# A scan with two MLPs on one core: the weights' VectorE work two stages behind ScalarE's, chunk inputs loaded at a period's front, a new token block's low parts and first products later

## The chip, the cores and the metric

The kernel runs on one core of a Trainium2 chip. Its engines run their own instruction streams in the order in which the program issues them: TensorE (PE; weight loads stand apart as PEld), VectorE (DVE), ScalarE (ACT), GpSimd (POOL) and SyncE (SP), which here issues nearly all DMA transfers. The metric is device time in microseconds (us) of one execution; lower is better.

## The reference

Three parts follow one another. A recurrence with a 40 x 40 state for each of 32 heads runs over 768 tokens; its output is the input of two MLPs with hidden width 2048 over 3072 tokens.

```python
for t in range(S):                               # B, H, S, D = 4, 8, 768, 40
    y[:, :, t] = np.einsum('bhd,bhde->bhe', rt, state)
    Sa = np.einsum('bhde,bhe->bhd', state, at)
    state_decay = state * wt[:, :, None, :] - np.einsum('bhd,bhe->bhde', Sa, bt)
    state = state_decay + np.einsum('bhd,bhe->bhde', vt, kt)
x = y.transpose(0, 2, 1, 3).reshape(B * S, H * D)        # 3072 x 320
h = x @ w_in                                     # 320 x 2048
x = (np.maximum(h, 0.0) ** 2) @ w_out            # 2048 x 320
h = x @ w_in2
out = (h * np.cos(h)) @ w_out2
```

The MLP weights come as 64-bit patterns of doubles and are turned into single precision on the chip.

## The kernel before, in words

**Chunks and periods.** The recurrence is cut into 12 chunks of 64 tokens. For each chunk the interaction of its tokens is a triangular system per head, which is solved; then the state moves on by matrix products. `Program.period(c)` is one period: a table of 42 slots says, with `at(slot, function, ...)`, what is issued when. Everything in a slot is written out in program order, and each engine takes its share in that order; nothing is reordered later.

A period holds work of several chunks. For chunk c, the state's products (`pq`, `px`, `pu`, `py`, `pm`) and the stores. For chunk c+1, the end of `gt` (products `pgt` on PE, masked by DVE into `ga`), `gt_out` (SP writes `ga` to DRAM as `Ls`, L445), `solve_load` in slot 6 (SP loads `T`, L458, and four pieces of `L` back from `Ls`, L461, then two `l`, L463), the solver from slot 9 to 36, `solve_store` (Tn, Ts) in slot 37 and `load_t` in slot 38. For chunk c+2, the inputs: `load_kb` (L362, the k and b inputs, 832 KB, into tile `cin`), `load_a` (L365, tile `at`), `compact_kb` (DVE multiplies kb by a scale in four pieces, `cin<-cin` 104x512, slots 10 to 16), `compact_a`, and the front of `gt`. For chunk c+3, `load_w` (L359, the decay inputs, also in `cin`) and the first scans of `decay`. The trace names both loads `cin`; the compaction and the scans of DVE stand under L144, the helper through which DVE's instructions go.

**The solver.** 31 pairs of `ttmp = T * L` (L472) and `T = T - ttmp` (L475), then a copy of the result (L478). From chunk 2 on it runs on POOL, one pair after another, with other POOL work between the pairs in the order of the program.

**The weights.** Class `Weights` turns a piece of weights over in stages that are one call apart: load `w` (SP), `clamp` (ACT, with DVE's max and min), `bits` (two DVE instructions), `add` (POOL, `u<-u,w`, L181), and an end that splits the piece or stores it (`w2f`, L281). In periods one call stands in every slot or every second slot.

**The MLPs.** A generator gives out MLP work in small steps (`yield`), about 1.5 per slot from period 2 on, and alone after the last period. For each token block and each of 16 weight tiles f it issues `h` (8 products from the high and low parts `xh`, `xl` of the block's input, L863), the activation (ACT `g`, `gh`; POOL the low part `gl` = g − gh, L720, two steps later by a list `later`), and, two tiles behind, `out(q-2)` (8 products into `po`, L819). A new block begins with `split_x`, which makes `xh` on ACT (L691) and `xl` on DVE. In the periods c = 4, 6, 8 and 10 a new block begins.

Of the kernel before, what the change touches and what calls it, by code (L numbers as in the profile page):

```python
# [15 lines left out]
ALU = mybir.AluOpType  # L16
# [103 lines left out]
def f32_of_bits(bits):  # L120
    return float(np.array([bits], np.uint32).view(np.float32)[0])
# [3 lines left out]
LOW_WORD, HIGH_WORD = f32_of_bits(0x38100000), f32_of_bits(0x47EFFFFF)  # L125
# [31 lines left out]
class Weights:  # L157
# [8 lines left out]
    def clamp(self, w, u):  # L166

        nc = self.nc
        nc.scalar.activation(u, w[:, :, 1].bitcast(F32), AF.Abs)  # L169
        nc.scalar.activation(w[:, :, 0], w[:, :, 0].bitcast(U32), AF.Copy, scale=2.0 ** -29)  # L170
        self.vec.tensor_scalar(u, u, LOW_WORD, HIGH_WORD, op0=ALU.max, op1=ALU.min)

    def bits(self, w, u):

        hi, ui = w[:, :, 1], u.bitcast(I32)
        self.vec.tensor_scalar(ui, ui, 0x07FFFFFF, 3, op0=ALU.bitwise_and, op1=ALU.logical_shift_left)
        self.vec.scalar_tensor_tensor(ui, hi, -0x40000000, ui, op0=ALU.bitwise_and, op1=ALU.bitwise_or)

# [69 lines left out]
    def pieces(self, nm, tiles, period, end):  # L248

        if not self.raw:  # L250
            return iter(())

        def job(f, c0, n):
            st = {}

            def load():
                st["w"] = self.p.tile([128, 256, 2], I32, tag="w", name="w", bufs=2)[:, 0:n]
                self.load(nm, f, st["w"], c0)

            def clamp():  # L260
                st["u"] = self.p.tile([128, 256], F32, tag="u", name="u", bufs=2)[:, 0:n]
                self.clamp(st["w"], st["u"])

            return [(0, load), (4, clamp), (5, lambda: self.bits(st["w"], st["u"])),
                    (6, lambda: self.add(st["w"], st["u"], st["u"])), (period + 5, lambda: end(f, c0, st["u"]))]

        return self.stages([job(f, *z) for f in tiles for z in PIECES], period)

# [376 lines left out]
class Mlp:  # L645
# [34 lines left out]
                    nc.sync.dma_start(xf[p0:p0 + n], self.x2s[bass.ds(blk, 1), r0:r0 + n].rearrange("o p t -> (o p) t"))  # L680
        self.xf[layer, self.key(blk)] = xs

    def split_x(self, layer, blk):

        nc = self.nc
        xs = self.xf.pop((layer, self.key(blk)))
        if self.xn is None:
            self.xn = [self.p2.tile([128, 3, 512], F32R, tag=nm, name=nm, bufs=1) for nm in ("xh", "xl")]
        xh, xl = self.xn
        for kt in range(3):  # L690
            nc.scalar.activation(xh[:, kt], xs[kt], AF.Copy)  # L691
            self.vec.tensor_tensor(xl[:, kt], xs[kt], xh[:, kt], op=ALU.subtract)

    def load_w2(self, f, src):

# [86 lines left out]
    def stream(self, blocks):  # L782


        self.later = []
        for z in self.pipeline(blocks):
            if z is None:
                self.later = [(n - 1, fn) for n, fn in self.later]
                while self.later and self.later[0][0] <= 0:
                    self.later.pop(0)[1]()  # L790
            yield z
        for _, fn in self.later:
            fn()

    def pipeline(self, blocks):
        nc = self.nc
        steps = [(layer, blk, f) for layer, blk in blocks for f in range(NF)]
        gs = {}

        def out(e):  # L800
            layer, blk, f = steps[e]
            if f == 0:
                self.pos = self.outputs(layer)
            gh, gl = gs.pop(e)
            wo = self.ws[layer, f][:, 640:SW]
            if layer:
                seq = [(j, gh, ws) for j in range(4) for ws in (0, 1)] + [(j, gl, 0) for j in range(4)]
                for k, (j, x, ws) in enumerate(seq):
                    nc.tensor.matmul(self.pos[j][:, 0:DM], x[:, 128 * j:128 * j + 128],  # L809
                                     wo[:, DM * ws:DM * ws + DM],  # L810
                                     start=(f == 0 and x is gh and ws == 0), stop=(f == NF - 1 and x is gl))
                    if f == NF - 1 and x is gl:
                        self.finish_tokens(blk, j)
                    if k % 2:
                        yield None
                return
            seq = [(0, 0, gh), (0, 3, gh), (1, 1, gh), (1, 4, gh), (2, 2, gh), (2, 2, gl), (0, 0, gl), (1, 1, gl)]
            for k, (m, ws, x) in enumerate(seq):
                nc.tensor.matmul(self.pos[m], wo[:, 128 * ws:128 * ws + 128], x,  # L819
                                 start=(f == 0 and k in (0, 2, 4)), stop=(f == NF - 1 and k in (5, 6, 7)))  # L820
                if k % 2 and k < 7:
                    yield None
            if f == NF - 1:
                self.finish(blk)
                self.done.add((layer, self.key(blk)))
            if self.w2 is not None and blk is blocks[-1][1] and f < self.loads:
                self.load_w2(f, self.w2)
            yield None

        def split_next(q):  # L830

            yield steps[q][:2]
            self.split_x(*steps[q][:2])
            nxt = blocks.index(steps[q][:2]) + 1
            if nxt < len(blocks) and (0, blocks[nxt][1]) in self.done and blocks[nxt][0]:
                self.load_x(*blocks[nxt])

        def ahead(q):
            if q + 2 < len(steps) and self.p3 is not None and steps[q + 2][0]:
                f = steps[q + 2][2]  # L840
                if (1, f) not in self.ws:
                    self.split_w2(f)

        for q in range(len(steps) + 2):
            if q < len(steps):
                layer, blk, f = steps[q]
                if q == 0:
                    yield layer, blk
                    self.split_x(layer, blk)
                    yield None  # L850
                if not layer:
                    ahead(q)
            if q >= len(steps):
                self.split_act()
                yield from out(q - 2)
            if q < len(steps):
                wi = self.ws[layer, f][:, 0:640].rearrange("p (k m) -> p k m", m=128)
                h = self.hidden(layer, q - steps.index((layer, blocks[0][1], 0)))
                xh, xl = self.xn
                seq = [(0, xh, 0), (0, xl, 0), (2, xh, 0), (1, xh, 1), (1, xl, 1),  # L860
                       (3, xh, 1), (4, xh, 2), (4, xl, 2)]
                for k, (ws, x, kt) in enumerate(seq):
                    nc.tensor.matmul(h, wi[:, ws], x[:, kt], start=(k == 0), stop=(k == 7))  # L863
                    if k % 2 and k < 7:
                        yield None
                if f == NF - 1 and q + 1 < len(steps):
                    yield from split_next(q + 1)
                gs[q] = []
                act = self.act(layer, h, gs[q])
                for _ in act:  # L870
                    ahead(q)
                    if f == 1:
                        break
                yield None
                if q >= 2:
                    yield from out(q - 2)
                for _ in act:
                    pass
# [26 lines left out]
class Program:  # L905
# [132 lines left out]
    def period(self, c):  # L1038

        A, nch = self.A, self.nch  # L1040
        more = c + 1 < nch
        st = [A.state(c, g) for g in range(4)]
        todo, rate = {}, {}

        def at(t, f, *args):
            todo.setdefault(t, []).append((f, args))
# [38 lines left out]
        if c + 2 < nch:  # L1085
            for t in (0, 2, 3, 4, 5, 6, 7, 9):
                at(t, step, self.dcs[c + 2])
            at(7, A.load_kb, c + 2)
            at(13, A.load_a, c + 2)
            ck = A.compact_kb(c + 2)  # L1090
            for t in (10, 12, 14, 16):
                at(t, step, ck)
            at(20, A.compact_a, c + 2, 0)
            at(28, A.compact_a, c + 2, 1)
            self.gts.setdefault(c + 2, A.gt(c + 2))
            for t in (24, 25, 26, 32, 33, 34, 36, 37, 38):
                at(t, step, self.gts[c + 2])
            at(37, A.gt_out, c + 2, 0, 0)
            at(39, A.gt_out, c + 2, 0, 1)
        if c + 3 < nch:  # L1100
            self.dcs[c + 3] = A.decay(c + 3)
            at(30, A.load_w, c + 3)
            for t in (34, 35, 36, 38, 40, 41):
                at(t, step, self.dcs[c + 3])
        for t in range(42):
# [114 lines left out]
```

## Time and profile before

| | before |
|---|---|
| median of 3 runs | 1269.22 us (1266.93 to 1270.55) |
| profiled execution, its own time | 1271.16 us |
| its span | 1269.3 us |
| mean granted TensorE clock | 0.905 of full speed |
| PE busy | 1071.2 us (84%) |
| DVE busy | 702.9 us (55%) |
| ACT busy | 696.4 us (55%) |
| POOL busy | 663.2 us (52%) |

The profiled execution is one run under the hardware profiler; the span is from its first to its last recorded instruction. Busy time is an average over a recurrence part (about the first 800 us, PE 50 to 100% busy) and an MLP part (the rest, PE nearly always busy), so the shares say little without the stretch that they come from. An idle time of an engine carries what ended it, as "[2.25 <-DMA L<-Ls]": 2.25 us idle, ended when that transfer landed.

### The profile page before, as it was taken

What the parts mean: (1) busy time and instruction counts of PE and PEld (TensorE: products, weight loads), DVE (VectorE), ACT (ScalarE), POOL (GpSimd) and SP (SyncE); (2) the same over time, 40 slices, a digit from 0 to 9 for tenths busy, and PEclk for the clock granted to TensorE, in tenths of its full rate; (3) what the DMA queues carried; (4) which work ended last, traced back from release to release, by engine and by line L of the source; (5) the groups of instructions that cost most, each with busy time, mean ns of one, the idle gap of its engine ahead of it and who ended that gap; (6) DMA issues with size and microseconds to landing.
All of it is one profiled execution on the core that took longest, in us unless ns stands there. A gap on an engine that the chain in (4) does not pass through costs nothing.

```text
span 1269.3 us, 26741 instructions
## 1 busy us (share of the span) xinstructions
PE 1071.2 (84%) x10242; PEld 900.0 (71%) x10242; DVE 702.9 (55%) x1378; ACT 696.4 (55%) x1444; POOL 663.2 (52%) x1043
## 2 busy tenths in 40 slices
PE   3245626788979898988988989999999999999997
PEld 3144525666757676867776767777889999999996
DVE  6869856666655565655564543124696343443432
ACT  4133633656655556654846466447756565655553
POOL 4112486595938382848484838126796333333332
PEclk9985655788988888988989889899999999999999
DMA  6473653637282727463747262236201010100000
GB/s 177 89 166 100 152 140 65 139 87 149 60 187 83 150 66 156 104 132 87 159 105 148 54 137 71 58 99 216 70 12 46 1 47 1 47 13 34 1 22 25
DMA packets 271952, 115.96 MB, mean 91 GB/s; under 512 B 229990, under 2 KB 250982, under 8 KB 270670
## 3 DMA queue, kind: packets, MB, share of 16 engines
q1 hardware_dynamic: 269979, 113.47, 37.6%
q8 instruction: 83, 1.36, 0.4%
q10 hardware_dynamic: 1834, 0.69, 0.2%
q14 instruction: 56, 0.45, 0.1%
HBM read 88.42 MB, written 25.69 MB: 90 GB/s over the span
## 4 chain that ended last, share of the span: by engine, by line
PE 48%; POOL 20%; DMA 11%; DVE 10%; issue 5%; SPq 4%; ACT 2%; POOLq 0%; ACTq 0%; DVEq 0%
PE h L863 21%; PE pt L809 13%; POOL T L475 7%; PE po L819 6%; POOL ttmp L472 6%; DMA cin<-cin 6%; POOL gl L720 3%; POOL u L181 2%; DMA xf<-xs 1%; PE px L597 1%; DVE T L475 1%; DVE ttmp L472 1%; DMA t<-Tn 1%; DVE cin L144 1%; PE pu L605 1%
## 5 line engine op out<-in xcount | busy, mean ns | idle before, releaser
L863 PE MATMUL h<-xh,ws 128*128 128x512 f32 x960 | 332.1, 409 | 20.2 <-ACT g L717 18.0
L863 PE MATMUL h<-xl,ws 128*128 128x512 f32 x576 | 234.9, 408 | 0.5 <-DVE xl L144 0.5
L863 PEld LDWEIGHTS h<-xh,ws 128*128 128x128 f32 x960 | 184.9, 194 | 62.6 <-ACT g L717 20.1
L748 POOL TENSOR_TENSOR gl<-g,gh 128x512 fp32r<-128x512 f32 x96 | 125.1, 1303 | 191.0 <-ACT gh L747 158.9
L720 POOL TENSOR_TENSOR gl<-g,gh 128x512 fp32r<-128x512 f32 x96 | 126.8, 1320 | 186.5 <-ACT gh L719 146.0
L819 PE MATMUL po<-gh,ws 128*128 128x512 f32 x480 | 143.1, 422 | 1.9 <-ACT o L767 1.3
L472 POOL TENSOR_TENSOR ttmp<-T,L 128x126 f32<-128x126 f32 (+22 forms) x310 | 124.1, 400 | 35.7 <-DMA L<-Ls 15.3
L475 POOL TENSOR_TENSOR T<-T,ttmp 128x126 f32<-128x126 f32 (+22 forms) x310 | 128.7, 415 | 20.1
L717 ACT ACTIVATE g<-h 128x512 f32<-128x512 f32 x96 | 57.2, 596 | 134.2 <-PE h L863 92.5
L809 PE MATMUL pt<-ws,gh 128*128 128x320 f32 x768 | 128.1, 308 | 0.5 <-DVE g L144 0.4
L863 PEld LDWEIGHTS h<-xl,ws 128*128 128x128 f32 x576 | 111.9, 194 | 21.3 <-DVE xl L144 1.1
L181 POOL TENSOR_TENSOR u<-u,w 128x384 int32<-128x384 int32 (+2 forms) x72 | 54.7, 760 | 136.9 <-DVE u L144 108.9
L809 PEld LDWEIGHTS pt<-ws,gh 128*128 128x128 f32 x768 | 119.9, 188 | 8.3 <-DVE g L144 0.6
L144 DVE SCALAR_TENSOR_TENSOR g<-n,h 128x512 f32<-128x512 int32 x96 | 66.0, 688 | 103.2 <-ACT n L728 100.4
L728 ACT ACTIVATE n<-h 128x512 int32<-128x512 f32 x96 | 57.3, 596 | 119.9 <-PE h L863 119.8
L431 PE MATMUL pgt<-at,cin 40*128 40x104 f32 x768 | 70.7, 325 | 51.8 <-DVE at L144 21.0
L819 PEld LDWEIGHTS po<-gh,ws 128*128 128x128 f32 x480 | 94.0, 202 | 25.9 <-ACT o L767 1.9
L144 DVE TENSOR_SCALAR u<-u 128x160 f32<-128x160 f32 (+9 forms) x144 | 50.5, 351 | 99.7 <-ACT u L169 88.9
L144 DVE TENSOR_TENSOR g<-g,h 128x512 f32<-128x512 f32 x96 | 65.8, 685 | 71.7 <-ACT g L732 71.7
L144 DVE TENSOR_TENSOR mov<-pu,kc 64x416 f32<-64x416 f32 x96 | 56.5, 588 | 83.8 <-PE pu L606 81.4
L431 PEld LDWEIGHTS pgt<-at,cin 40*128 40x128 f32 x768 | 60.9, 226 | 58.6 <-issue 24.3
L819 PE MATMUL po<-gl,ws 128*128 128x512 f32 x288 | 85.9, 402 | 0.0
(104 smaller groups left out, 2310.2 us busy)
## 6 DMA issues: line engine op xcount, KB each, us to landing
w<-moe SPq DMA_DIRECT2D x20, 704.0 KB
rv<-rv SPq DMA_DIRECT2D x48, 256.0 KB
cin<-cin SPq DMA_DIRECT2D x11, 832.0 KB
Ls<-ga SPq DMA_DIRECT2D x48, 128.0 KB
L<-Ls SPq DMA_DIRECT2D x48, 128.0 KB
cin<-cin SPq DMA_DIRECT2D x11, 422.5 KB
at<-cin SPq DMA_DIRECT2D x11, 416.0 KB
mov<-vt SPq DMA_DIRECT2D x96, 40.0 KB
```

What stands on the lines that cost most here:

```text
L144: fn(*args, **kwargs)
L181: self.nc.gpsimd.tensor_tensor(t.bitcast(I32), u.bitcast(I32), w[:, :, 0], op=ALU.add)
L431: nc.tensor.matmul(pv[par][:, j], self.kb[r0:r0 + 40, p0 + j].rearrange("p h b -> p (h b)"), self.at[r0:r0 + 40, p0 + j], start=True, stop ...
L472: eng.tensor_tensor(tv, T[:, 0:r, j:j + 1].to_broadcast([128, r, n]), L[:, j:j + 1, j + 1:32].to_broadcast([128, r, n]), op=ALU.mult)
L475: eng.tensor_tensor(T[:, 0:r, j + 1:32], T[:, 0:r, j + 1:32], tv, op=ALU.add)
L717: nc.scalar.activation(g, h, AF.Relu)
L720: self.later.append((2, lambda: nc.gpsimd.tensor_tensor(gl, g, gh, op=ALU.subtract)))
L728: nc.scalar.activation(n, h, AF.Copy, bias=0.25, scale=float(np.float32(1.0 / (2.0 * np.pi))))
L748: nc.gpsimd.tensor_tensor(gl, g, gh, op=ALU.subtract)
L809: nc.tensor.matmul(self.pos[j][:, 0:DM], x[:, 128 * j:128 * j + 128], wo[:, DM * ws:DM * ws + DM], start=(f == 0 and x is gh and ws == 0), ...
L819: nc.tensor.matmul(self.pos[m], wo[:, 128 * ws:128 * ws + 128], x, start=(f == 0 and k in (0, 2, 4)), stop=(f == NF - 1 and k in (5, 6, 7)))
L863: nc.tensor.matmul(h, wi[:, ws], x[:, kt], start=(k == 0), stop=(k == 7))
```

## The change

Four things move; the number of instructions of each kind stays.

1. In `Weights`, DVE's max/min goes from `clamp` to `bits`, so that `clamp` holds ACT's two instructions alone. In `pieces`, `bits` goes from stage 5 to 6 and `add` from 6 to 7; the end stays at `period + 5`. In the two other users of `clamp` DVE's max/min comes with `bits`, one step after ACT or more.
2. `load_kb` goes from slot 7 to 1, `load_a` from 13 to 11, `load_w` from 30 to 18.
3. A new block of layer 0 makes its low parts `xl` four steps later, as a job of the list `later`, of which now every due job runs.
4. For the first tile of a new block of layer 0 (not the first of all), `out(q-2)` is issued before `h`'s products and not behind them.

```diff
     def clamp(self, w, u):
         nc.scalar.activation(w[:, :, 0], w[:, :, 0].bitcast(U32), AF.Copy, scale=2.0 ** -29)
-        self.vec.tensor_scalar(u, u, LOW_WORD, HIGH_WORD, op0=ALU.max, op1=ALU.min)
     def bits(self, w, u):
         hi, ui = w[:, :, 1], u.bitcast(I32)
+        self.vec.tensor_scalar(u, u, LOW_WORD, HIGH_WORD, op0=ALU.max, op1=ALU.min)
         self.vec.tensor_scalar(ui, ui, 0x07FFFFFF, 3, op0=ALU.bitwise_and, op1=ALU.logical_shift_left)
...
-            return [(0, load), (4, clamp), (5, lambda: self.bits(st["w"], st["u"])),
-                    (6, lambda: self.add(st["w"], st["u"], st["u"])), (period + 5, lambda: end(f, c0, st["u"]))]
+            return [(0, load), (4, clamp), (6, lambda: self.bits(st["w"], st["u"])),
+                    (7, lambda: self.add(st["w"], st["u"], st["u"])), (period + 5, lambda: end(f, c0, st["u"]))]
...
-    def split_x(self, layer, blk):
+    def split_x(self, layer, blk, wait=0):
...
         for kt in range(3):
             nc.scalar.activation(xh[:, kt], xs[kt], AF.Copy)
-            self.vec.tensor_tensor(xl[:, kt], xs[kt], xh[:, kt], op=ALU.subtract)
+            if not wait:
+                self.vec.tensor_tensor(xl[:, kt], xs[kt], xh[:, kt], op=ALU.subtract)
+        if wait:
+            def low():
+                for kt in range(3):
+                    self.vec.tensor_tensor(xl[:, kt], xs[kt], xh[:, kt], op=ALU.subtract)
+
+            self.later.append((wait, low))
...
-                while self.later and self.later[0][0] <= 0:
-                    self.later.pop(0)[1]()
+                due = [fn for n, fn in self.later if n <= 0]
+                self.later = [z for z in self.later if z[0] > 0]
+                for fn in due:
+                    fn()
...
-            self.split_x(*steps[q][:2])
+            self.split_x(*steps[q][:2], 0 if steps[q][0] else 4)
...
             if q < len(steps):
+                if f == 0 and q and layer == 0:
+                    yield from out(q - 2)
...
-                if q >= 2:
+                if q >= 2 and (f or layer):
                     yield from out(q - 2)
...
-            at(7, A.load_kb, c + 2)
-            at(13, A.load_a, c + 2)
+            at(1, A.load_kb, c + 2)
+            at(11, A.load_a, c + 2)
...
-            at(30, A.load_w, c + 3)
+            at(18, A.load_w, c + 3)
```

The order of SP's issues from the front of period c=9 to its a load, before (`cin<-cin 104x2048` is the kb load, `L<-Ls` what the solver reads, `w` and `w2f` are weights):

```order
L445 DMA Ls<-ga 64x8x64
L534 DMA rv<-rv 128x512
L185 DMA w<-moe 128x512
L281 DMA w2f<-u 128x160
L445 DMA Ls<-ga 64x8x64 x2
L534 DMA rv<-rv 128x512
L542 DMA mov<-vt 64x4x40 x2
L458 DMA T<-kti 128x512
L461 DMA L<-Ls 32x32x32 x4
L463 DMA l_119<-Ls 32x16x32 x2
L362 DMA cin<-cin 104x2048
```

and SP at the same place in the changed kernel:

```order
L445 DMA Ls<-ga 64x8x64
L362 DMA cin<-cin 104x2048
L534 DMA rv<-rv 128x512
L185 DMA w<-moe 128x512
L281 DMA w2f<-u 128x160
L445 DMA Ls<-ga 64x8x64 x2
L534 DMA rv<-rv 128x512
L542 DMA mov<-vt 64x4x40 x2
L458 DMA T<-kti 128x512
L461 DMA L<-Ls 32x32x32 x4
L463 DMA l_119<-Ls 32x16x32 x2
L365 DMA at<-cin 104x16x64
```

The kb load has moved from behind L and l to a place ahead of rv, w, two Ls writes, mov, T and L.

DVE in period c=9 around the first pieces of the compaction, before (`cin<-cin 104x512` is a piece, `u` the weights, the rows between are the state's):

```order
L144 TENSOR_TENSOR cin<-cin 104x512
L144 TENSOR_SCALAR u<-u 128x256
L144 TENSOR_TENSOR MT_111<-py,MT_111 104x160
...
L144 TENSOR_TENSOR yt<-sz,lam_93 104x256
L144 TENSOR_TENSOR cin<-cin 104x512
L144 TENSOR_SCALAR u<-u 128x256
L144 SCALAR_TENSOR_TENSOR u<-w,u 128x256
L144 TENSOR_TENSOR cin<-cin 104x512
```

and DVE at the same place in the changed kernel:

```order
L144 TENSOR_TENSOR cin<-cin 104x512
L144 TENSOR_TENSOR MT_111<-py,MT_111 104x160
...
L144 TENSOR_TENSOR yt<-sz,lam_93 104x256
L144 TENSOR_TENSOR cin<-cin 104x512 x2
L144 TENSOR_SCALAR u<-u 128x256 x2
L144 SCALAR_TENSOR_TENSOR u<-w,u 128x256
```

The first `u` row (max and min) now stands directly ahead of the other two, behind three pieces of the compaction and the state's rows.

POOL from the end of one solver run (L478) into the next, at the new block of period c=6, before:

```order
L478 COPY L<-T 64x512
L720 TENSOR_TENSOR gl<-g,gh 128x512
L181 TENSOR_TENSOR u<-u,w 128x160
L720 TENSOR_TENSOR gl<-g,gh 128x512 x2
L472 TENSOR_TENSOR ttmp<-T,L 128x31
L475 TENSOR_TENSOR T<-T,ttmp 128x31
L472 TENSOR_TENSOR ttmp<-T,L 128x30
L475 TENSOR_TENSOR T<-T,ttmp 128x30
L472 TENSOR_TENSOR ttmp<-T,L 128x58
```

and POOL at the same place in the changed kernel:

```order
L478 COPY L<-T 64x512
L727 TENSOR_TENSOR gl<-g,gh 128x512
L181 TENSOR_TENSOR u<-u,w 128x160
L727 TENSOR_TENSOR gl<-g,gh 128x512
L472 TENSOR_TENSOR ttmp<-T,L 128x31
L475 TENSOR_TENSOR T<-T,ttmp 128x31
L472 TENSOR_TENSOR ttmp<-T,L 128x30
L475 TENSOR_TENSOR T<-T,ttmp 128x30
L472 TENSOR_TENSOR ttmp<-T,L 128x58
L727 TENSOR_TENSOR gl<-g,gh 128x512
```

The third `gl` (L720 before, L727 in the changed kernel) has moved from ahead of the solver's first pair to behind the start of its third.

## Rows read from the trace of the kernel before

**Rows 1.** The page: span; busy time; chain by line; kb's issues and KB.

```profile
span 1269.3 us, 26741 instructions
...
PE 1071.2 (84%) x10242; PEld 900.0 (71%) x10242; DVE 702.9 (55%) x1378; ACT 696.4 (55%) x1444; POOL 663.2 (52%) x1043
...
PE h L863 21%; PE pt L809 13%; POOL T L475 7%; PE po L819 6%; POOL ttmp L472 6%; DMA cin<-cin 6%; POOL gl L720 3%; POOL u L181 2%; DMA xf<-xs 1%; PE px L597 1%; DVE T L475 1%; DVE ttmp L472 1%; DMA t<-Tn 1%; DVE cin L144 1%; PE pu L605 1%
...
cin<-cin SPq DMA_DIRECT2D x11, 832.0 KB
```

**Rows 2.** Windows: us, busy (count) by engine, PE clock, DMA share, GB/s.

```profile
133.73:157.14 23.41, 16.65 (x296) 14.48 (x290) 19.86 (x41) 16.03 (x40) 12.21 (x16) 0.68 0.85 187
...
670.47:690.77 20.30, 19.96 (x323) 15.85 (x323) 11.79 (x27) 15.79 (x36) 5.30 (x5) 1.00 0.82 161
...
sum 224.90, PE 187.53 PEld 152.42 DVE 129.36 ACT 150.07 POOL 57.34; mean PE 18.75 PEld 15.24 DVE 12.94 ACT 15.01 POOL 5.73
...
sum 433.65, PE 368.16 PEld 295.26 DVE 254.08 ACT 231.80 POOL 363.78; mean PE 36.82 PEld 29.53 DVE 25.41 ACT 23.18 POOL 36.38
...
870.00:1269.30 399.30, 390.22 (x2117) 349.34 (x2115) 194.92 (x275) 228.44 (x379) 185.29 (x162) 0.99 0.10 36
```

**Rows 3.** Timeline of SP, front of period c=9: start, us, what, count.

```profile
677.63 0.57 SPq L534 DMA_DIRECT2D rv<-rv  x1
...
683.86 4.53 SPq L461 DMA_DIRECT2D L<-Ls  x4
...
689.67 0.45 SPq L362 DMA_DIRECT2D cin<-cin  x1
...
691.81 4.86 SPq L542 DMA_DIRECT2D mov<-vt  x1
```

**Rows 4.** Timeline of POOL: start, us, what [idle before <- releaser].

```profile
164.61 1.02 POOL L181 TENSOR_TENSOR u<-u,w 128x384 int32<-128x384 int32 x1 [4.36 <-DVE u L144]
...
690.77 0.24 POOL L472 TENSOR_TENSOR ttmp<-T,L 128x31 f32<-128x31 f32 x1 [2.25 <-DMA L<-Ls]
...
701.09 1.12 POOL L181 TENSOR_TENSOR u<-u,w 128x256 int32<-128x256 int32 x1 [3.50 <-DVE u L144]
```

**Rows 5.** Waits: who waits <- for whom: us in total, times, longest.

```profile
POOL gl L720 <- ACT gh L719: 146.0, 35, 16.2
POOL u L181 <- DVE u L144: 108.9, 22, 22.4
...
DVE cin L144 <- DMA cin<-cin: 59.4, 12, 7.2
...
PE pm L638 <- DVE MT L144: 37.5, 15, 12.9
```

**Rows 6.** Timeline of DVE, in period 0 and in period c=9.

```profile
94.09 0.69 DVE L144 TENSOR_TENSOR cin<-cin 104x512 f32<-104x512 f32 x1 [5.30 <-DMA cin<-cin]
...
689.50 0.42 DVE L144 TENSOR_TENSOR lam<-lam 104x252 f32<-104x252 f32 x1
696.46 0.70 DVE L144 TENSOR_TENSOR cin<-cin 104x512 f32<-104x512 f32 x1 [6.54 <-DMA cin<-cin]
...
700.59 0.43 DVE L144 SCALAR_TENSOR_TENSOR u<-w,u 128x256 int32<-128x256 int32 x1
```

**Rows 7.** Timeline of SP: the L issues in the setup, at c=6 and at c=10.

```profile
29.11 8.06 SPq L461 DMA_DIRECT2D L<-Ls  x4
...
497.11 2.88 SPq L461 DMA_DIRECT2D L<-Ls  x4
...
749.64 3.05 SPq L461 DMA_DIRECT2D L<-Ls  x4
```

**Rows 8.** Timeline of POOL ahead of the solver's start at c=6 and c=10.

```profile
503.45 1.28 POOL L720 TENSOR_TENSOR gl<-g,gh 128x512 fp32r<-128x512 f32 x1 [3.25 <-ACT gh L719]
...
754.74 1.30 POOL L720 TENSOR_TENSOR gl<-g,gh 128x512 fp32r<-128x512 f32 x1 [2.12 <-ACT gh L719]
```

**Rows 9.** Timeline of PE at the new block in the tail.

```profile
849.00 0.50 PE L863 MATMUL h<-xh,ws 128*128 128x512 f32 x1 [1.99 <-ACT xh L691]
```

## The prediction

> **What bounds the kernel now.** I read the page first: TensorE (PE) is busy 1071.2 of 1269.3 us, and the chain that ended last holds, beside PE's own lines, POOL's solver lines (L472, L475), 6% of "DMA cin<-cin" and 2% of "POOL u L181" [rows 1]. So there are stretches in which PE is not the limit. The windows say which. From 870 us on, in the two MLP layers, PE is busy 390.22 of 399.30 us at a granted clock of 0.99: that part is fixed work, and the change issues none of it away. The periods of the recurrence, ahead of it, fall into two kinds of stretch. In the ten runs of the solver on GpSimd (POOL), from the first `ttmp` to the copy of L478, 433.65 us in all, POOL is busy 363.78 and PE 368.16. In the ten stretches from that copy to the next first `ttmp`, 224.90 us, POOL is busy only 57.34, and the DMA engines are 82 to 85% busy in the two that I show [rows 2]. So a period is a loop: solver run (POOL's work and its waits), then a chain of issues on SyncE (SP) and of transfers which ends with `L<-Ls`, on which the next run waits. In period c=9 that is SP's L issue from 683.86 for 4.53 us [rows 3], and the first `ttmp` at 690.77 after 2.25 us of idle time, released by DMA L<-Ls [rows 4]: 2.38 us after the last L issue ended (688.39).
>
> What stretches a solver run is read from the waits: POOL's adds of the weights (u L181) waited 108.9 us for VectorE (DVE), and DVE's compaction of the inputs (cin) waited 59.4 us for the DMA of cin, 12 times, up to 7.2 [rows 5]. The two hang together. In period c=9 the kb load of cin is issued at 689.67, after L [rows 3]. DVE stands at `cin<-cin` from about 689.9 and starts at 696.46 after 6.54 us; behind it in DVE's queue stands the rest of the weights' `u`, which ends at 701.0 [rows 6]; and POOL, in the middle of the solver, stands 3.50 us at the add that needs it [rows 4].
>
> **The change, part by part.** Δ below is the time by which L lands later in a period.
>
> *The waits in the solver runs.* There are eight waits of POOL's add for DVE's `u` inside the runs, from 4.36 us at 164.61 to 3.50 at 701.09; their sum is 22.7 [rows 4]. The change acts twice on them: kb comes some 12 us earlier (its new place is ahead of `rv` at 677.63 instead of 689.67 [rows 3]), so that `cin<-cin` finds its data, and the add comes a stage later behind DVE's work. I take all away: −22.7. In period 0 the solver runs on DVE itself and stood 5.30 us behind the same `cin<-cin` at 94.09 [rows 6]: −5.3. Of POOL's waits for ScalarE's gh [rows 5] five lie in solver runs and make 6.0 us; DVE's late rows also hold up PE (pm waited 37.5 us for DVE's MT [rows 5]) and so h, g and gh, but I can't tie each to cin: half, −3.0, with 0 and −6.0 as bounds.
>
> *The kb load ahead of L.* 832 KB go into the stretch where the DMA engines are busiest, some seven issues ahead of L. Upper bound of Δ: the whole transfer, 832 KB [rows 1] or 851,968 bytes at 161 GB/s [rows 2], 5.3 us, and 0.45 for SP's issue [rows 3], 5.7. Lower bound: the engines have (1 − 0.82) · 20.30 = 3.7 us to spare in such a stretch [rows 2]; at 187 GB/s the load takes 4.6, so 0.9 stays, about 1. The nearest row is the setup, where kb is issued right ahead of T and L: there the four L issues took 8.06 us [rows 7], against 4.53 in period c=9 [rows 3], so +3.5. Here some 6 us of issues lie between kb and L, in which part of kb drains, so I take **Δ = 2.5**, below the setup's 3.5 and well above the free share's 1. It counts in ten periods (c = 0 to 9, which have a chunk c+2). In one of them, c=6, L isn't what the start waits for: its issues ended at 499.99 [rows 7], so by c=9's 2.38 us it landed at about 502.4, and the start at 504.7 followed a gl of 1.28 us that began at 503.45 [rows 8]; there Δ costs only what exceeds 2.3, since that gl goes away (next part). Together 9 · 2.5 + 0.2 = +22.7. Starts where POOL's own work ended just before are counted in full, the dear side.
>
> *The new token block.* At c = 4, 6, 8 and 10, h's first products come after out(q−2) and the low parts later. The order on POOL shows the third `gl` of the stretch move from before the run into it: 1.28 us each [rows 8], four times +5.1. At c=10 the start at 756.0 had followed such a gl (754.74 and 1.30 [rows 8]); L's issues ended at 752.69, landing by the same 2.38 at 755.1 [rows 7]: −0.9. In the tail the one block change at 849.00 left PE idle 1.99 us for xh [rows 9]; out's eight products now fill it: −1.8. Sum of the part: +2.4.
>
> *Costed at nothing.* The counts of instructions stay. DVE's max/min and the add a stage later: hidden by a `pieces` job's last step, which stays at period + 5; a w load needs the add two jobs before, now one or more slots ahead of it still. If that cover goes, SP stands at a w load, and with it everything queued behind (Ls, T, L): as dear as Δ. The a load two slots earlier and the w65 load twelve earlier fall into solver runs, where the transfers have room; kb no longer stands there, and the `mov` issue which took 4.86 us behind it [rows 3] should be free, but who waits for it is PE, which isn't the limit there.
>
> **Sum.** −22.7 − 5.3 − 3.0 + 22.7 + 2.4 = −5.9, against the profiled execution's 1271.16: 1265.3. That execution lies 1.9 above the median of the three runs, 1269.22, so I forecast **1263**. As a formula for the runs: 1238.3 + 10 Δ. No change is at Δ = 3.1. What a measurement of this kernel can tell is about 0.3%, 3.8 us: faster below Δ = 2.7, slower above 3.5.
>
> On what stands ahead in a queue: the setup row shows four issues stretched by 3.5 us behind kb [rows 7], not by all of the kb's time. The Trainium skill, page "DMA: Bandwidth & Descriptors", section "Queues, rings and completion order", says that on each SDMA engine descriptors are consumed in the order of their ring. By that, all of kb would go ahead of Ls and L however the engines' free time falls; what it would give is the second rival.
>
> **The rivals.**
> *kb is hidden* (Δ of 1.5 or less). For it: engines 15 to 18% free [rows 2], and seven issues between. L's landing also waits for the Ls writes and SP's own rate of one issue per 0.6 us, so a delay of the bytes may not be one of the chain. Against it: the setup's 8.06. Time: 1238.3 + 10 to 15, about 1248 to 1253; with all of gl's 6.0 us gone, 1245.
> *kb goes wholly ahead* (Δ of 3.5 or more; slower). Place: the rings, at Ls (x2) and L behind kb. For it: the 82 to 85% share, and `mov`, which stood 4.86 us behind kb in period c=9 [rows 3]. Against it: it takes the ring to be still full when L is issued 6 us later. At Δ = 3.9 it gives 1277, at 5.3 about 1291; from 3.1 on it decides the sign. The rule just named is this case at 5.3; the setup's 3.5 speaks for less.
> *No change.* The waits go, but something else takes their place: PE, which has 368.16 us of work in 433.65 of the runs [rows 2], or DVE's work inside them, so that POOL waits elsewhere. Against it: a run of 43.4 us less 3.3 leaves 40.1, above PE's mean of 36.8. Price: the runs keep their length, and Δ about 1 is paid back by the stretches: about 1269.
>
> **How the numbers follow.** Likeliest case, Δ between 1.5 and 3.5: 0.50, its own range 1253 to 1273; of it 0.32 is faster by over 0.3%, 0.16 within, 0.02 slower. kb hidden: 0.20, all faster. kb wholly ahead: 0.22, of which 0.20 slower and 0.02 within. No change: 0.08, within. Together faster 0.52, same 0.26, slower 0.22. The range of eight in ten: from 1246 (kb hidden with all of gl's waits gone) to 1277 (Δ = 3.9), leaving some 0.05 below and 0.15 above.
>
> **What would show it.** In the changed kernel: DVE's wait for the DMA of cin (59.4) falls to under 10, and POOL's u L181 inside the runs to under 5; the ten runs' sum falls from 433.65 to about 413 (with the gls that move in). The stretches between grow from 224.90 by Δ in most, to about 244; SP's L issue in period c=9 takes 6 to 8 us instead of 4.53. If the runs stay long with no wait at u, the third rival is right; if the stretches stay at 225, the first; at 260 and more, the second. What would make me wrong outright: a w load that waits for a late add and stops SP ahead of L, which the trace of before can't show.

## The result and the profile after

The changed kernel is slower: 1287.13 us, median of 4 runs (1284.36 to 1288.31), against 1269.37 (1266.93 to 1270.55, 4 runs with the three above); ratio 1.0137, 95% interval 1.0119 to 1.0154. The forecast was 1263, with a range up to 1277. The profiled execution took 1286.07 us, its span is 1284.0. Two single executions further down, which ran at a lower granted TensorE clock (1511.53 us with the weights alone, 1311.09 with the order of products alone), are left out of medians and ratios.

The page of the changed kernel, the lines that answer to [rows 1]:

```profile
span 1284.0 us, 26719 instructions
...
PE 1074.4 (84%) x10242; PEld 900.6 (70%) x10242; DVE 712.9 (56%) x1378; ACT 697.4 (54%) x1444; POOL 667.4 (52%) x1043
...
PE h L874 23%; PE pt L818 13%; PE po L828 9%; POOL T L475 4%; POOL ttmp L472 4%; DMA xf<-xs 3%; DVE lam L144 2%; POOL gl L727 2%; DMA Ls<-ga 2%; DMA cin<-cin 2%; PE pgt L431 2%; DVE cin L144 2%; DMA t<-Tn 2%; DVE u L144 2%; DVE T L475 1%
```

"DMA cin<-cin" has gone from 6% to 2% of the chain and "POOL u L181" from the line. So the waits at which the change aims mostly left the chain, and still the end came later. The windows (columns as in [rows 2]): the stretch ahead of the solver in period c=9, the sum of the ten stretches, the sum of the ten solver runs, and the last 399.3 us:

```profile
686.55:709.15 22.60, 19.68 (x283) 15.63 (x281) 12.43 (x25) 13.79 (x32) 4.77 (x6) 0.85 0.88 179
...
sum 248.96, PE 181.79 PEld 147.51 DVE 126.53 ACT 132.16 POOL 53.48; mean PE 18.18 PEld 14.75 DVE 12.65 ACT 13.22 POOL 5.35
...
sum 422.48, PE 373.74 PEld 298.13 DVE 264.90 ACT 250.82 POOL 371.29; mean PE 37.37 PEld 29.81 DVE 26.49 ACT 25.08 POOL 37.13
...
884.70:1284.00 399.30, 390.44 (x2118) 349.63 (x2116) 196.29 (x276) 228.63 (x380) 185.36 (x162) 0.99 0.10 35
```

The stretches grew by 24.1 us (forecast 19), the runs shrank by 11.2 only (forecast 20.6); the end of the kernel runs as before. The waits that answer to [rows 5]:

```profile
POOL gl L727 <- ACT gh L726: 143.6, 27, 21.1
...
POOL u L181 <- DVE u L144: 79.5, 14, 22.5
ACT ws L208 <- POOL u L181: 74.4, 22, 15.6
...
DVE cin L144 <- DMA cin<-cin: 7.9, 2, 7.6
```

DVE's wait for the kb transfer fell from 59.4 to 7.9 as forecast, POOL's for u by 29.4. Inside the ten solver runs (their windows one by one) POOL's waits for u went from 22.7 us to none, while those of gl for gh rose from 6.0 to 10.6. Period c=9 on SP, to set against [rows 3]:

```profile
693.61 0.54 SPq L362 DMA_DIRECT2D cin<-cin  x1
...
698.65 3.19 SPq L542 DMA_DIRECT2D mov<-vt  x2
...
703.47 3.42 SPq L461 DMA_DIRECT2D L<-Ls  x4
```

From the kb issue's start to the end of L's issues 13.28 us pass; before, from the same place, then rv's (677.63), it was 10.76: +2.5 here. The delay doesn't stand within the L issues (3.42, before 4.53), as I had expected, but ahead of them. What SP waits for in this stretch:

```profile
SPq L542 <- DMA cin<-cin: 2.0, 1, 2.0
SPq L461 <- DMA Ls<-ga: 0.9, 2, 0.6
```

The second of the two `mov` (3.19 us together, before 1.23) is the eighth issue behind kb, and SP stands at it for 2.0 us until kb itself has landed. Then L's issue waits for the Ls writes, which went out behind kb. Over the whole kernel SP waits for kb in this way four times, 9.9 us in all, each time at the eighth issue behind it (a `mov`, a `T` or an `Ls`); before it never did. L's waits for Ls in the kernel before, and then, in the changed kernel, these and the three other waits for kb:

```profile
SPq L461 <- DMA Ls<-ga: 2.7, 4, 0.9
...
SPq L461 <- DMA Ls<-ga: 13.9, 11, 3.7
...
SPq L458 <- DMA cin<-cin: 5.1, 2, 3.3
...
SPq L445 <- DMA cin<-cin: 2.8, 1, 2.8
```

### The profile page after: what moved, and what is told of

Read it like the earlier page. It is cut to its first block, busy times and chain, and to the rows that moved or that the text cites. A ratio compares the mean times of both kernels' runs of the same rounds, so it can differ in the third digit from the quotient of the medians.

```text
span 1284.0 us, 26719 instructions
## 1 busy us (share of the span) xinstructions
PE 1074.4 (84%) x10242; PEld 900.6 (70%) x10242; DVE 712.9 (56%) x1378; ACT 697.4 (54%) x1444; POOL 667.4 (52%) x1043
## 4 chain that ended last, share of the span: by engine, by line
PE 56%; POOL 13%; DVE 11%; DMA 10%; SPq 4%; ACT 3%; issue 3%; POOLq 0%; ACTq 0%; DVEq 0%
PE h L874 23%; PE pt L818 13%; PE po L828 9%; POOL T L475 4%; POOL ttmp L472 4%; DMA xf<-xs 3%; DVE lam L144 2%; POOL gl L727 2%; DMA Ls<-ga 2%; DMA cin<-cin 2%; PE pgt L431 2%; DVE cin L144 2%; DMA t<-Tn 2%; DVE u L144 2%; DVE T L475 1%
## 5 line engine op out<-in xcount | busy, mean ns | idle before, releaser
L874 PE MATMUL h<-xh,ws 128*128 128x512 f32 x960 | 330.6, 407 | 17.8 <-ACT g L724 17.4
L727 POOL TENSOR_TENSOR gl<-g,gh 128x512 fp32r<-128x512 f32 x96 | 127.0, 1323 | 203.8 <-ACT gh L726 143.6
L874 PEld LDWEIGHTS h<-xh,ws 128*128 128x128 f32 x960 | 183.3, 192 | 61.1 <-ACT g L724 21.6
L475 POOL TENSOR_TENSOR T<-T,ttmp 128x126 f32<-128x126 f32 (+22 forms) x310 | 131.4, 424 | 19.5
L431 PE MATMUL pgt<-at,cin 40*128 40x104 f32 x768 | 72.0, 332 | 52.0 <-DVE at L144 21.8
L181 POOL TENSOR_TENSOR u<-u,w 128x384 int32<-128x384 int32 (+2 forms) x72 | 56.8, 788 | 98.9 <-DVE u L144 79.5
## 6 DMA issues: line engine op xcount, KB each, us to landing
cin<-cin SPq DMA_DIRECT2D x11, 422.5 KB
```

Of the source, the lines that this page charges most:

```text
L181: self.nc.gpsimd.tensor_tensor(t.bitcast(I32), u.bitcast(I32), w[:, :, 0], op=ALU.add)
L431: nc.tensor.matmul(pv[par][:, j], self.kb[r0:r0 + 40, p0 + j].rearrange("p h b -> p (h b)"), self.at[r0:r0 + 40, p0 + j], start=True, stop ...
L475: eng.tensor_tensor(T[:, 0:r, j + 1:32], T[:, 0:r, j + 1:32], tv, op=ALU.add)
L727: self.later.append((2, lambda: nc.gpsimd.tensor_tensor(gl, g, gh, op=ALU.subtract)))
```

## The experiments

A ratio is to the kernel before on the same chip, where its runs had medians of 1269.8 to 1270.6. Each kernel is before with one part changed, where nothing else is said.

**The early kb load alone.**

```diff
-            at(7, A.load_kb, c + 2)
+            at(1, A.load_kb, c + 2)
```

> Only the kb load moves (slot 7 to 1); all else as before. Theory A (the early kb load delays L): the stretches between solver runs grow by some 3 us each, +25 to +30 in all, while DVE's waits for cin and most of POOL's waits for u go (runs -20 or so with period 0), so 1272 to 1280, between before and after. Rival B (the loss lies in the new token block's order): kb alone pays, 1250 to 1262.

Measured 1277.31 us, ratio 1.0040 (1.0016 to 1.0064). Sums of its stretches and of its runs:

```profile
sum 249.72, PE 182.69 PEld 147.34 DVE 126.39 ACT 136.77 POOL 56.30; mean PE 18.27 PEld 14.73 DVE 12.64 ACT 13.68 POOL 5.63
...
sum 416.23, PE 368.96 PEld 294.84 DVE 266.46 ACT 245.97 POOL 368.91; mean PE 36.90 PEld 29.48 DVE 26.65 ACT 24.60 POOL 36.89
```

and the solver's two groups on POOL (count, busy us, mean ns, idle before and what ended it), before and then here:

```profile
L475 POOL TENSOR_TENSOR T<-T,ttmp 128x126 f32<-128x126 f32 (+22 forms) x310 | 128.7, 415 | 20.1
...
L472 POOL TENSOR_TENSOR ttmp<-T,L 128x126 f32<-128x126 f32 (+22 forms) x310 | 124.1, 400 | 35.7 <-DMA L<-Ls 15.3
...
L475 POOL TENSOR_TENSOR T<-T,ttmp 128x126 f32<-128x126 f32 (+22 forms) x310 | 129.7, 418 | 20.1
L472 POOL TENSOR_TENSOR ttmp<-T,L 128x126 f32<-128x126 f32 (+22 forms) x310 | 128.1, 413 | 45.2 <-DMA L<-Ls 11.0 <-DMA l<-Ls 10.3 <-DMA at<-cin 3.6
```

The stretches grew by 24.8, and the one ahead of DVE's solver in period 0 by 4.3 (18.1 to 22.4); the last one, without kb, shrank by 0.9. So Δ is (24.8 + 0.9 + 4.3) / 10 = 3.0. The runs lost 17.4, period 0's solver 5.4. Theory A holds, B falls. The waits inside the ten runs fell from 28.7 to 6.3, that is by 22.4, 5 more than the runs; the same 310 pairs of the solver took 5.0 us longer on POOL. SP waited for kb's landing four times, 10.0 us in all, again at the eighth issue behind it, and at L's issue 14.8 us for Ls (before 2.7). That is 22.1 us more than before, to set beside the 29.1 by which the stretches grew, period 0's with them.

**Half the bytes.** As the last one, with the first 1024 of 2048 columns, in every period and in the setup.

```diff
-        self.nc.sync.dma_start(self.cin[:, W65:WK], self.i["cin"][c, :, W65:WK])
+        self.nc.sync.dma_start(self.cin[:, W65:W65 + 1024], self.i["cin"][c, :, W65:W65 + 1024])
```

> The kb load in slot 1 as in the run that moved it alone, but only its first 1024 of 2048 columns are loaded (the other half of the k and b inputs keeps old values, so the output isn't the reference's). Theory (the bytes ahead of L on busy DMA engines are the price): the growth of the stretches halves, from 25 to about 12 us over ten, and the time falls from 1277 to 1260 to 1266. Rival (the place in SP's queue is the price, one more issue and its waits): the stretches stay some 25 longer, 1274 to 1279.

Measured 1250.10, ratio 0.9851 (0.9825 to 0.9877), beyond what the theory expected and on its side; but the setup's solver also ends 3.4 us earlier here, since its load is halved too, and that has nothing to do with the place of the load. Its stretches:

```profile
sum 228.49, PE 170.44 PEld 138.05 DVE 118.90 ACT 132.25 POOL 55.91; mean PE 17.04 PEld 13.80 DVE 11.89 ACT 13.22 POOL 5.59
```

They grew by 3.6 (period 0's by 2.6, the last shrank by 0.9): Δ = 0.7. So one more issue at this place in SP's queue doesn't cost the 3.0; the bytes do, and not in proportion: the first 416 KB cost 0.7 us a period, the second 2.3. SP's waits show one way in which they cost: for kb's landing SP waits 1.3 us in all instead of 10.0, L's issue for Ls 10.1 instead of 14.8. The lower bound's free share doesn't give these numbers (nothing for the half, 0.9 for the whole). The mean granted TensorE clock is also higher here, 0.937 against 0.913, and some of the shorter stretches may be that; what part, this run doesn't show. Whether L would be spared SP's wait for kb with fewer than eight issues between the two was not tried.

**The compaction later, the kb load where it was.**

```diff
-            for t in (10, 12, 14, 16):
+            for t in (14, 16, 18, 20):
                 at(t, step, ck)
```

> The kb load stays at slot 7; instead DVE's compaction of it moves from slots 10, 12, 14, 16 to 14, 16, 18, 20, so that DVE doesn't reach it before it has landed. Theory (DVE's wait for kb is what stretched the runs, and the early load only paid for it in the stretches): DVE's wait for the DMA of cin falls from 59 to under 20, the runs by some 18 to 25, the stretches stay at 225: 1243 to 1254. Rival (PE takes the place of the wait in the runs): the wait goes, but the time stays within 1262 to 1270.

Measured 1246.38 (1242.07 to 1249.77), ratio 0.9795 (0.9747 to 0.9843): the lowest median of all. Its stretches and its runs:

```profile
sum 219.69, PE 167.98 PEld 137.15 DVE 119.00 ACT 134.80 POOL 56.29; mean PE 16.80 PEld 13.71 DVE 11.90 ACT 13.48 POOL 5.63
...
sum 422.95, PE 375.61 PEld 300.37 DVE 268.19 ACT 247.33 POOL 372.23; mean PE 37.56 PEld 30.04 DVE 26.82 ACT 24.73 POOL 37.22
```

and two of its waits:

```profile
DVE cin L144 <- DMA cin<-cin: 15.2, 7, 7.2
PE pm L638 <- DVE MT L144: 6.0, 5, 4.1
```

The wait for cin falls to 15.2 and PE's for MT from 37.5 to 6.0, the runs lose 10.7, and the stretches lose 5.2 where the early load made them grow. The time is in the theory's range, but not by its split: with period 0's 5.5 the runs lose 16.2 and not 18 to 25, since POOL's pairs take 8.0 us longer here, and another 5.1 us are gained behind the last run, where nothing was moved. There, before and then here, with the same 601 products of PE:

```profile
792.28:870.00 77.72, 70.95 (x601) 55.06 (x600) 18.83 (x33) 40.69 (x76) 21.80 (x17) 0.93 0.35 99
...
772.20:844.80 72.60, 66.84 (x601) 51.82 (x600) 18.40 (x34) 41.04 (x76) 22.11 (x17) 1.00 0.39 107
```

The clock of TensorE has two levels, 1.2 and 2.4 GHz; here it was at the upper one throughout (1.00); before it was at the lower one for a part (0.93), and PE's products took 4.1 us longer. The mean granted clock of the whole is 0.925 against 0.905, so some of the gain is the clock's; why it rose, this run doesn't show. The wait was worth removing, then: the compaction four slots later in DVE's queue takes most of it away, and the early load bought the same thing at ten times 3.0 us.

**The weights' stages alone** (item 1 of the change).

> Only the weights' stages move (DVE's three instructions together, one stage later, POOL's add one stage later). Theory (POOL's wait for u is DVE standing at cin, so a later add shortens it but doesn't remove it): POOL u in the runs falls from 22.7 to some 8 to 15, 1255 to 1264. Rival (u now stands behind more pieces of the compaction, so the wait stays or grows): 1268 to 1275.

Measured 1276.96, ratio 1.0044 (1.0022 to 1.0066); slower than either range. Its waits:

```profile
POOL gl L727 <- ACT gh L726: 170.3, 35, 15.7
...
POOL u L181 <- DVE u L144: 114.5, 21, 22.8
ACT ws L208 <- POOL u L181: 81.9, 24, 15.0
...
DVE cin L144 <- DMA cin<-cin: 57.8, 12, 8.6
```

u didn't fall [rows 5], ScalarE's split `ws` waits 17.9 longer for POOL's add (64.0 before) and gl 24.3 longer for gh. The loss lies in the ten solver runs, 438.9 us against 433.7, where gl's waits for gh went from 6.0 to 14.6 and those for u only from 22.7 to 21.6. SP, too, stands longer at a weight load that needs POOL's add; before, here, and in the changed kernel:

```profile
SPq L185 <- POOL u L181: 59.1, 13, 9.9
...
SPq L185 <- POOL u L181: 96.1, 15, 12.3
...
SPq L185 <- POOL u L181: 120.9, 18, 12.1
```

Four kernels took this apart. First, the last step of a piece at period + 6, so that the split is as far behind the add as before:

```diff
-                    (7, lambda: self.add(st["w"], st["u"], st["u"])), (period + 5, lambda: end(f, c0, st["u"]))]
+                    (7, lambda: self.add(st["w"], st["u"], st["u"])), (period + 6, lambda: end(f, c0, st["u"]))]
```

> The weights' stages alone as changed, but the last step of a piece at period + 6, one stage later too. Theory (ScalarE's split stands at POOL's later add and holds up gh, so gl): ACT's wait ws for POOL's u goes back from 82 to about 64, gl's wait from 170 to about 146, and the time from 1277 to 1269 to 1273. Rival (the cost comes through DVE, whose three instructions now stand together behind the compaction): no change, 1275 to 1279.

```profile
POOL gl L727 <- ACT gh L726: 177.1, 38, 15.8
...
ACT ws L208 <- POOL u L181: 65.5, 21, 15.5
```

Measured 1277.72, ratio 1.0069 (1.0050 to 1.0087). The split's wait went back as meant, and SP's at the weight load to 68.5; gl's wait and the time did not: the theory of the split falls, and SP's stand at the weights isn't the price either. Then max and min alone in the later step (stages 5 and 6 as before), and the stages alone (max and min with the clamp, bits at 6, add at 7):

> Of the weights' part only DVE's max and min go from the clamp to the later step; the stages of the bits and of POOL's add stay at 5 and 6. Theory (the later add and the later bits cost, not the place of max and min): 1268 to 1272. Rival (three DVE instructions together right ahead of POOL's add make it wait longer): 1274 to 1280.

> Of the weights' part only the stages: bits at 6 and POOL's add at 7, with DVE's max and min still right behind ScalarE's clamp. Theory (the later add is what costs: the stand moves from the add to the next gl): 1274 to 1279, as the whole part. Rival (max and min later is needed for the loss too): 1268 to 1272.

Max and min alone: 1271.38, ratio 1.0010 (0.9988 to 1.0031), no difference that can be told. The stages alone: 1273.85, just under the range of the theory, ratio 1.0034 (1.0009 to 1.0060). By their middles the later stages (of bits and of the add together) carry most of the loss; the intervals of the two overlap, so that is likely and not shown. And the changed kernel with the weights as before:

> The changed kernel with the weights' stages and max/min as before; loads and block stay changed. Theory (the weights' later stages cost by themselves): the time falls by some 5 to 7 us, 1279 to 1283. Rival (they cost only where DVE stands at cin, which the early kb load has ended): no difference, 1285 to 1289.

Measured 1279.09, ratio 1.0096 (1.0067 to 1.0124): 8.0 us below the changed kernel by the medians, 5.2 by the ratios, whose intervals just overlap. So the part probably costs by itself, also where DVE no longer stands at cin.

**The new token block alone** (items 3 and 4), then of it only the order of products (low parts at once).

> Only the new token block moves (low parts four steps later, out before h for the first tile). Theory A+ (the third gl moves behind the solver's start and waits there for a late gh): the solver runs of periods 4, 6, 8, 10 grow by some 3 to 4 us each, so 1278 to 1286. Rival (moving the block costs only the gl's own 1.28 us each, as forecast, and the tail's gap is filled): 1270 to 1273. Rival (block's loss comes only together with the early kb load): 1265 to 1270.

> Of the new block's change only the order of products (out before h for the first tile); the low parts are made at once as before. Theory (the third gl moves behind the solver's start through the order of products): the same loss as the whole block part, +3 to +5, 1272 to 1276. Rival (the low parts' delay is what costs): 1267 to 1270.

Measured 1274.41, ratio 1.0018 (0.9990 to 1.0047), and 1273.1, ratio 1.0014 (0.9990 to 1.0037): each by itself can't be told from no change, nor the one from the other, and the times lie between the ranges. The four runs of the block's part grew by 5.0 us together, about the forecast's 1.28 each and not the 3 to 4 of the theory. In the changed kernel with the block as before:

> The changed kernel with the new token block as before; loads and weights stay changed. Theory (the block's part costs by itself): the time falls by 3 to 9 us, 1278 to 1284, and the runs of periods 4, 6, 8, 10 by some 2 us each. Rival (it costs nothing here): 1285 to 1289.

Measured 1278.10, ratio 1.0089 (1.0060 to 1.0117): 9.0 below the changed kernel by the medians, 6.1 by the ratios. The four runs of periods 4, 6, 8 and 10 take 167.9 us in the changed kernel and 160.4 here, 7.5 less, as expected; but its ten stretches take 255.4 against 249.0, so that most of it is given back there. The two profiled executions are 5.0 apart in their spans, and 3.7 of that lies behind the last run (473.8 us against 477.5), of which the run doesn't show the cause.

**Parts upon the late compaction.** The block's part, and the weights' part:

> The new block's part as changed, upon the kernel with the compaction in slots 14 to 20. Theory (the third gl behind the solver's start costs by itself, some 2 us in each of four runs): the runs of periods 4, 6, 8 and 10 grow by 1 to 2.5 us each and the time is 1248 to 1253. Rival (that too hangs on DVE's standing): 1244 to 1247.

> The weights' stages as changed, upon the kernel with the compaction in slots 14 to 20. Theory (the weights' part costs 6 us only where DVE stands at cin, since the three instructions and the state's rows queue behind it): 1243 to 1249, no difference to 1246.4. Rival (the part costs by itself, by later adds): 1251 to 1255.

The block: 1258.06 (1251.08 to 1261.30), 11.7 above the late compaction alone and more than the theory had. Its four runs are together also 11.7 longer (4.1, 3.4, 2.2, 2.0), but that the two numbers agree is chance: the profiled execution is one of the shorter ones (1252.44), and its stretches lose 3.2. On POOL at c=4 there:

```profile
358.60 0.28 POOL L472 TENSOR_TENSOR ttmp<-T,L 128x58 f32<-128x58 f32 x1
361.73 1.28 POOL L727 TENSOR_TENSOR gl<-g,gh 128x512 fp32r<-128x512 f32 x1 [2.84 <-ACT gh L726]
```

The moved gl costs its 1.28 and 2.84 of waiting there. The weights: 1249.40 (1246.56 to 1251.67), 3.0 above, inside the scatter of both, and between the two expectations. The whole change with kb in slot 7, the compaction in slots 14 to 20 and `load_w` in slot 22:

> The changed kernel with the kb load back in slot 7, the compaction in slots 14, 16, 18, 20 and the w load of the inputs in slot 22 (behind the last piece of the compaction, which reads the same tile); weights' stages and the new block as changed. Theory (the parts add): 1246 plus 6.5 for the weights and 3.8 for the block, 1254 to 1259. Rival (the weights' stages cost only where DVE stands at cin, so without that wait they cost nothing): 1247 to 1252.

Measured 1251.97 (1250.15 to 1254.03), 5.6 above the late compaction alone and at the upper end of the rival's range: the parts don't add up to the theory's 1254 to 1259. That it is below the block's part by itself can't be told (ratios 0.9852 to 0.9885 and 0.9869 to 0.9939). Last, kb in slot 11 and the compaction in slots 16 to 22:

> The kb load in slot 11, behind the solver's start, and the compaction in slots 16, 18, 20, 22. Theory (bytes of kb that start right behind L's issue still hold up L's landing a little): the stretches shrink by up to 0.5 us each, 1240 to 1246. Rival (L has landed by then, and the later kb brings DVE's wait for cin back): 1246 to 1256.

Measured 1247.80 (1245.10 to 1250.91), no difference to 1246.38 that could be told: a kb load right behind L's issues, in slot 7, costs L nothing measurable.

## Why the prediction was wrong

**Where the error lies.** The sum was −5.9, and the span grew by 14.7. Ahead of the solver, period 0 included, the two profiled executions show +29.0 where +21.8 stood (22.7 and the block's −0.9); in the solver runs −15.4 where −25.9 stood (−31.0, and 5.1 for the moved gls); in the rest +1.1 where −1.8 stood. So half of the 20.6 us is what the solver runs didn't give back, and a third lies in the stretches ahead of them.

**"I take Δ = 2.5."** The mechanism was right, the size was not: 3.0 with the kb load alone, so +29.1 in its stretches ahead of the solver where +22.7 stood. The setup's 3.5 was the better row. "In which part of kb drains" was too hopeful: SP itself stands until kb has landed, and L's issue until Ls has, 22.1 us of waiting more than before. I had named the Ls writes only as a reason for a hidden load. The lower bound, the engines' free share, was the wrong measure: it gave about 1. Of the 4.86 us of `mov` that I had put down to kb in the rivals, 2.6 were a wait for PE's `po`. The Trainium skill, page "DMA: Bandwidth & Descriptors", section "Queues, rings and completion order", has descriptors of one engine consumed in ring order; the case that I had set beside it was 5.3, and 3.0 was measured.

**"I take all away: −22.7", "−5.3" and "half, −3.0".** Together −31.0; with kb alone −22.8 was measured. The waits did go (22.4 of 28.7 in the runs, 5.4 us in period 0). What stood in their place is POOL itself: 5.0 us more for the same pairs, since DVE, which had stood idle beside the solver, now works at the same time. This is the term that I had taken as pure gain. In the whole change the pairs take only 2.1 us more; there the waits of gl for gh, of which I had taken half away, rose by 4.6, and the moved gls came on top.

By these two the kb load alone ends at +6.3 in its span (29.1 less 22.8), and 6.0 is what its span shows (1275.3). My sum had −8.3 for it.

**"Costed at nothing" for the weights.** It cost 5.6 us alone, by the ratio, and 5 to 8 in the whole. The cover that I named (the last step stays) isn't the point, as the run at period + 6 shows. I counted the later add as a help for the waits at u, and no help was there: as long as DVE stands at cin, u waits nearly the same, and when it doesn't, there is nothing to remove. The sign that I gave for being wrong outright, SP standing at a w load for a late add, did come (59.1 to 120.9 us; 79.3 with the old weights), but with that wait taken back to 68.5, in the run at period + 6, the time stayed. What the price is stays open. Alone, the loss lies in the runs, with gl's longer waits for gh; in the changed kernel these are 10.6 us against 2.8 with the old weights, and yet the ten runs are equally long (422.5 and 422.4). Nor is gl's wait summed over the kernel a measure: it rises as much by the kb load alone (171.0 from 146.0), where it falls inside the runs (4.6 from 6.0).

**"The new token block": +2.4.** "1.28 us each" was about right for the part alone (5.0 us in four runs), but too low a price in the changed kernel, where the four runs are 7.5 longer by it: the gl in the run also waits for its gh, 2.79 us at c=4, 2.90 at c=6, 1.53 at c=8 and 0.29 at c=10. The tail's −1.8 came and mostly went: the wait of 1.99 [rows 9] is gone there, but the next `po` waits longer for o, 2.73 us against 1.29.

**A wait that I had nowhere.** A new block's inputs xf are loaded behind kb. ACT's waits for them, before, with kb alone, and in the changed kernel:

```profile
ACT xh L691 <- DMA xf<-xs: 12.4, 9, 5.3
...
ACT xh L691 <- DMA xf<-xs: 26.4, 11, 6.0
...
ACT xh L691 <- DMA xf<-xs: 26.5, 12, 5.7
```

So this belongs to the kb load and not to the block's part. PE and ACT of the changed kernel at c=6:

```profile
501.87 0.63 ACT L691 ACTIVATE xh<-xf 128x512 fp32r<-128x512 f32 x1 [5.46 <-DMA xf<-xs]
...
507.20 1.54 ACT L528 ACTIVATE tt<-pt 32x256 f32<-32x256 f32 x4
...
507.61 0.60 PE L605 MATMUL pu<-xsb,tt 64*64 64x104 f32 x2 [6.35 <-ACT tt L528]
```

ACT stands at xh for xf, `tt` is queued behind it, and PE stands 6.35 us at `pu`. At the same place before ACT had stood 5.2 us in three waits, and PE 4.90, so that at c=6 only some 2 us are new.

**The rivals.** The second (kb wholly ahead) named the right place and the right sign, but its mechanism, Δ = 3.9 and more, isn't what happened: Δ is 3.0, just below the 3.1 that I gave as the break-even, and the rest of my error lies in the three terms that I had counted as gains or nothing. The third, that something takes the place of the waits, was right in part: POOL's slower pairs, gl's waits, and in period c=9 PE itself, busy all 37.24 us of the run. Its "less 3.3" a run follows from none of my sums; 20.6 over ten runs is 2.1, and the argument against it is the same with that.

In numbers from parts alone: kb +5.1, weights +5.6, block +2.3, by their ratios, 13 of the 17.4 that the whole ratio gives; taken out of the whole, by ratios too, the weights give back 5.2 and the block 6.1. Each of these can be 3 to 4 us more or less, so it isn't shown that the parts hurt each other. The two other loads (a and w65) were not tried alone.

## What to carry to other kernels

Where an engine stands at a transfer, look first whether its instruction can come later in its queue: here four numbers in a table won 2%, part of it by the clock. Moving the transfer earlier puts its bytes ahead of something else. Ask which later issue of the same queue waits for it to land, and which transfer of the chain reads what was written behind it; if the chain that sets the period runs through that stretch, charge these waits in every period. The free share of the DMA engines gave a third of the price here. A wait that leaves one engine's queue is not a gain until the next instruction in that queue is ready: read what that one waits for.

## What the hardware showed that I had not expected

POOL's tensor operations take longer while DVE runs beside them. In period c=9 of the kernel before, DVE stood idle from 689.92 to 696.46 [rows 6], and POOL ran the 128x81 pair so:

```profile
693.52 0.33 POOL L472 TENSOR_TENSOR ttmp<-T,L 128x81 f32<-128x81 f32 x1
693.92 0.34 POOL L475 TENSOR_TENSOR T<-T,ttmp 128x81 f32<-128x81 f32 x1
```

In the changed kernel DVE (`cin<-cin`, two pieces from 711.78 for 1.53 us) and POOL at the same pair:

```profile
711.78 1.53 DVE L144 TENSOR_TENSOR cin<-cin 104x512 f32<-104x512 f32 x2
...
712.09 0.66 POOL L472 TENSOR_TENSOR ttmp<-T,L 128x81 f32<-128x81 f32 x1
712.84 0.87 POOL L475 TENSOR_TENSOR T<-T,ttmp 128x81 f32<-128x81 f32 x1
```

1.53 us for the two instead of 0.67. The second ends at 713.71, some 0.4 us after DVE's pieces (713.31), as if it had begun only then. It holds for all 310 pairs: measured against the median of their shape where no DVE instruction overlaps them, the overlapped ones take 29.3 us longer in the kernel before (394 of 620) and 34.2 with the kb load alone (430), and the others come out at the median. The difference, 4.9, is the 5.0 us of the kb load alone. The Trainium skill, page "SBUF — State Buffer", section "SBUF: two separate sides", says that DVE and GpSimd share a port pair under an exclusive lock, which a DVE operation with two inputs in SBUF takes for its whole length; these rows agree. So work that comes back to DVE during a solver run on POOL is paid for in part by POOL.
